# Two layers of cached attention and gated MLP on one core: the first pair's q computed ahead by columns, the softmax scale moved into exp, w_down in 2 KB runs, one more cache unit held, new tables

## The chip, the cores and the metric

The kernel runs on one core of one Trainium2 chip. The metric is the device time of one execution in microseconds; the time before is the median of three runs. A profiled execution of the same program gives the trace. Its engines are called PE (matrix multiply; PEld is its weight load), DVE, ACT, POOL and SP, and SP issues every DMA of this kernel.

## The reference

Four sequences of one token each (B = 4, D = 512) pass twice through the same pair of blocks with the same weights and caches:

```python
x = x + A(layernorm(x)); x = x + B(layernorm(x))     # layer 1
x = x + A(layernorm(x)); x = x + B(layernorm(x))     # layer 2

# A: attention, 32 query heads, 8 cache heads of 4096 x 128
q = (x @ wq).reshape(B, 1, 32, 128).transpose(0, 2, 1, 3)
scores = einsum("bhqd,bhkd->bhqk", q, repeat(k_cache, 4)) * 128 ** -0.5
o = einsum("bhqk,bhkd->bhqd", softmax(scores), repeat(v_cache, 4))
return o.reshape(B, 1, 4096) @ wo
# B: gated MLP, F = 1792
return einsum("bsf,fd->bsd", sigmoid(x @ w_gate) * (x @ w_up), w_down)
```

All inputs are bf16. A cache head of one batch is 1 MB of K and 1 MB of V. The caches are 64 MB in all and do not fit beside the weights, so what layer 2 needs of them is read again unless it was held on the chip.

## The kernel before, in words

**Units and pairs.** A unit is one cache head of one batch in one layer: 2 x 4 x 8 = 64 units. Two neighbouring heads make a pair, so there are 32 pairs. `ORDER` lists the pairs by layer, batch and pair of heads. Pairs of layer 2 of one batch are mixed with pairs of layer 1 of others. Pair g holds units 2g and 2g+1.

**Slots and loads.** Twelve slots of 1 MB hold K or V of a unit. The function `pump` issues the next loads of a fixed list on SP as long as a slot is free (L402), and the parts of the weights wo, w_gate, w_up and w_down in between (L388). `LOADS` sets how K and V alternate in that list. SP takes its list in order, so a load that waits for its slot holds up all behind it. A K slot is given back by the unit's scores, a V slot by its pv. `RET` names, for each batch, heads whose K or V stay in their slots from layer 1 to layer 2 and are not read again: 30 units of 1 MB, so that 98 of 128 cache loads remain.

**A step.** The plan has 33 steps. Step k does the scores and the softmax of pair k and the second product of pair k-1:

- `k_turn` (L848): a unit's K is turned in its slot by a DVE stream transpose, whole (2.3 us) or in halves.
- `q_blocks` (L660, POOL): q of the pair is spread into a block pattern, qz.
- `scores` (L863, PE): 16 matmuls for each unit of the pair. The first unit's are issued in the step before, at the place that `FIRST_AT` names.
- `smax`, `spread_max` (L886, L897), `softmax` (L906 DVE, L914 ACT exp with a bias pointer, L928 POOL), `sums`, `inverse` (L937, L947).
- `ptrans` (L959 PE): the turn of the probabilities, and 16 ACT copies out of PSUM (L982).
- `pv` (L999, PE): 32 matmuls a unit; `normalise` (L1059 DVE); `wo_mm`, `wo_add` (L1077, L1097).

`STEP` holds three small choices for each step: when the first K is turned, whether the first pv goes ahead of the softmax, whether the second K is turned in halves.

**A pass.** When all eight heads of a batch in layer 1 are done, the batch goes through its MLP and on to q of layer 2, while steps of other batches go on. The pass has 18 pieces (`pass_steps`): LayerNorm in three pieces (`ln_a` L507, `ln_b_sum` L573, `ln_b_rs`, the last a Newton iteration for the reciprocal root on DVE), the gate product (`wide_mm`, L676), tanh, the up product, the product of both, `down` (L795), `down_add` (L807), LayerNorm again, then q. q comes as rows: `q_row` (L746), two groups of 16 matmuls with 512 columns; `q_out` brings them out of PSUM with the LayerNorm scale on it (L759 on ACT, L766 on DVE); `q_half` (L776) and `q_turn` (L785) turn them into columns; `q_spread` (L635 PE, L646 ACT) copies them to where POOL reads them. `PLACES` holds one (step, place) for each piece of each batch. A step has nine places, 0 to 8. The last piece also frees the first pair of layer 2: its `q_blocks` is put there, and the first unit's scores at place 8.

**The tail.** After the last pair, all four batches go through the MLP of layer 2 together: `wide_mm` 112 times, `down_rows` (L1299), and one output DMA (L1338).

The weights of `wide_mm` are taken so:

```python
lhsT=wsb[:, k, fc * P:(fc + 1) * P],
```

Of the kernel before, what the change touches and what calls it, by code (L numbers as in the profile page):

```python
# [12 lines left out]


RET = [
    {"k": (0, 5, 6, 7), "v": (4, 5, 6, 7)},
    {"k": (4, 5, 6, 7), "v": (4, 5, 6, 7)},
    {"k": (4, 5, 6, 7), "v": (6, 7)},
    {"k": (0, 1, 2, 6, 7), "v": (0, 1, 6)},
]  # L20

ORDER = [
# [1 line left out]
    (0, 0, (0,)),  # L24
    (0, 0, (2,)),
    (0, 0, (3,)),
    (0, 2, (0,)),
    (0, 1, (1,)),
    (0, 1, (0,)),
    (1, 0, (3,)),  # L30
    (1, 0, (2,)),
    (0, 1, (2,)),
    (0, 1, (3,)),
    (1, 0, (1,)),
    (1, 0, (0,)),
    (0, 2, (1,)),
    (1, 1, (2,)),
    (1, 1, (3,)),
    (0, 2, (3,)),
    (0, 2, (2,)),  # L40
    (1, 1, (1,)),
    (1, 1, (0,)),
    (0, 3, (2,)),
    (1, 2, (3,)),
    (0, 3, (1,)),
    (0, 3, (0,)),
    (0, 3, (3,)),
    (1, 2, (2,)),
    (1, 2, (0,)),
    (1, 2, (1,)),  # L50
    (1, 3, (3,)),
    (1, 3, (0,)),
    (1, 3, (1,)),
    (1, 3, (2,)),
]

PLACES = [
    (
        (1, 8), (2, 0), (2, 0), (2, 0), (2, 0), (2, 0),
        (2, 1), (2, 3), (2, 5), (2, 6), (3, 0), (3, 2),  # L60
        (3, 2), (3, 5), (3, 5), (3, 5), (3, 6), (3, 6),
    ),
    (
        (1, 8), (2, 1), (2, 2), (2, 2), (2, 2), (2, 5),
        (2, 5), (2, 6), (2, 7), (2, 7), (3, 0), (3, 2),
        (3, 2), (3, 2), (3, 5), (3, 5), (3, 6), (3, 6),
    ),
    (
        (1, 8), (2, 0), (2, 1), (2, 2), (2, 2), (2, 2),
        (2, 2), (3, 0), (3, 1), (3, 1), (3, 2), (3, 2),  # L70
        (3, 5), (3, 5), (3, 5), (3, 5), (3, 6), (3, 6),
    ),
    (
        (1, 8), (1, 8), (1, 8), (1, 8), (2, 0), (2, 2),
        (2, 2), (2, 4), (2, 4), (2, 7), (3, 0), (3, 0),
        (3, 0), (3, 0), (3, 0), (3, 2), (3, 5), (3, 5),
    ),
]


FIRST_AT = (
    1, 2, 4, 1, 2, 2, 2, 2,
    2, 2, 2, 2, 2, 8, 7, 2,
    1, 3, 2, 4, 5, 5, 7, 4,
    4, 3, 2, 1, 2, 2, 7,
)

LOADS = (
    "kkvkkk", "", "", "kkvvkkvvvkkv", "kv", "kvk", "vkkvvk", "",
    "kvvvvvkk", "kv", "", "kkkvvkkvv", "k", "kvvkvv", "vk", "",  # L90
    "vkkvkkkkvv", "kkvkvvv", "kvk", "", "kvkvvvvkvvk", "", "kvkv", "",
    "", "kkvkvvkkkkvvkv", "kkvvv", "", "", "vvkkkvkkv", "", "vkvkv",
    "vvv",
)


STEP = (
    9, 3, 4, 9, 3, 9, 7, 0,
    6, 6, 6, 6, 0, 6, 6, 6,
    6, 6, 6, 0, 5, 6, 10, 6,  # L100
    6, 0, 6, 0, 1, 6, 0, 0,
    0,
)


# [101 lines left out]
def bass_interleave_layers__gqa_block_cached__glu_gated_glu__decode_kernel(  # L207
# [17 lines left out]
    P = 128  # L225
# [41 lines left out]
    rm_sb = [[small[:, 6 + 2 * i + t:7 + 2 * i + t] for t in range(2)] for i in range(2)]  # L267
    sm_sb = [[small[:, 10 + 3 * i + t:11 + 3 * i + t] for t in range(3)] for i in range(2)]
    blk_f = small[:, 16:20]
    ones_w = ones_f.broadcast_to([P, P])  # L270
    ident_bf = sbt([P, P], dt.bfloat16, "ident_bf")
    head_b = sbt([P, 2 * REP], dt.bfloat16, "head_b")
# [6 lines left out]
    xc_sb = sbt([P, KD, Bn], dt.float32, "xc")  # L279
    sq_sb = sbt([P, KD + 1, Bn], dt.float32, "sq")  # L280
    newt = sbt([P, 9, Bn], dt.float32, "newt")
    lnsum, _, vpe, nt_a, nt_b, nt_c, nt_y, rs = [newt[:, i, :] for i in range(8)]
    y0i = newt[:, 8, :].bitcast(dt.int32)
    xc_bf = sbt([P, KD, Bn], dt.bfloat16, "xc_bf")
    qT_sb = sbt([P, HQ * Bn], dt.bfloat16, "qT")
    qc_sb = sbt([P, Bn, HKV, NT4, REP], dt.bfloat16, "qc")
# [9 lines left out]
    pidx = qc_f[:, P:P + 32]  # L296
    half_f = qc_f[:, P + 32:P + 64]
    head_s = qc_f[:, P + 64:P + 64 + 2 * REP]
    QC = [f"qc{b}" for b in range(Bn)]
    gs_sb = pe_f[:, 0:KF * Bn]  # L300
    t_sb = pe_f[:, 64:64 + KF * Bn]
    hT_bf = qT_sb[:, 0:KF * Bn].rearrange("p (k b) -> p k b", b=Bn)
# [47 lines left out]
    for k, kinds in enumerate(LOADS):  # L350
        for o in range(2):
# [5 lines left out]
            if 2 * k + o >= 3 and w_small:  # L357
# [9 lines left out]
                         A_wo[n * REP * P:(n + 1) * REP * P, :].rearrange("(h p) n -> p h n", p=P)),  # L367
        "wg": lambda n: (wg_sb[:, n, :], B_w_gate[n * P:(n + 1) * P, :]),
        "wu": lambda n: (wu_sb[:, n, :], B_w_up[n * P:(n + 1) * P, :]),
        "wd": lambda n: (wd_sb[:, n * KH:(n + 1) * KH, :],  # L370
                         B_w_down[n * KH * P:(n + 1) * KH * P, :].rearrange("(k p) n -> p k n", p=P)),
    }
    assert KF == 2 * KH
    wkeys = {"wg": [f"wg{k}" for k in range(KD)], "wu": [f"wu{k}" for k in range(KD)], "wd": ["wd0", "wd1"]}
# [254 lines left out]
    def q_spread(b0, nb):  # L629
        N = HQ * nb  # L630
        fns = []
        for t in range(NT4):
            for a in range(4):
                fns.append(
                    (lambda t, a: lambda e: e.matmul(  # L635
                        M_ps[1][32 * a:32 * a + 32, t * N:(t + 1) * N],
                        lhsT=ident_bf[:, bass.ds(64 * (t // 2) + t % 2, 32, step=2)],
                        rhs=qT_sb[:, 0:N],
                        start=True,
                        stop=True,  # L640
                    ))(t, a)
                )
        S.group("pe", fns, reads=["qT"] + IDENT, writes=["M1"])
        for bi in range(nb):
            act(
                (lambda bi: lambda e: e.activation(  # L646
                    qc_sb[:, b0 + bi, :, :, :],
                    M_ps[1][:, 0:NT4 * N].rearrange("p (t u r b) -> p u t r b", t=NT4, u=HKV, r=REP)[:, :, :, :, bi],
                    ACTF.Copy,
                ))(bi),  # L650
                reads=["M1"],
                writes=[f"qc{b0 + bi}"],
            )

    def q_blocks(g):
        _, b, u = seq[2 * g]
        z = g % 2
        S.inst(
            "pool",
            lambda e: e.tensor_tensor(  # L660
                qz_sb[z][:, :, 0:4 * REP].rearrange("p i (a r) -> p i a r", r=REP),
                qc_sb[:, b, u:u + 2, :, :].rearrange("p u t r -> p (u t) r").unsqueeze(2).broadcast_to([P, 8, 4, REP]),
                blk_f.unsqueeze(1).unsqueeze(3).broadcast_to([P, 8, 4, REP]),
                ALU.mult,
            ),
            reads=[f"qc{b}", "blk"],
            writes=[f"qz{z}"],
        )

    def wide_mm(nb, which, f0, f1, M, mk):  # L670
        wsb, keys = ((wg_sb, wkeys["wg"]), (wu_sb, wkeys["wu"]))[which]
        fns = []
        for fc in range(f0, f1):
            for k in range(KD):
                fns.append(
                    (lambda fc, k: lambda e: e.matmul(  # L676
                        M[:, 64 + fc * nb:64 + (fc + 1) * nb],
                        lhsT=wsb[:, k, fc * P:(fc + 1) * P],
                        rhs=xc_bf[:, k, 0:nb],
                        start=(k == 0),  # L680
                        stop=(k == KD - 1),
                    ))(fc, k)
                )
        S.group("pe", fns, reads=["xcb"] + keys, writes=[mk])
# [71 lines left out]
    def q_out(h):  # L756
        if h == 0:
            act(
                lambda e: e.activation(row_sb[:, :], M_ps[0][:, :], ACTF.Copy, scale=rs[:, 0:1]),  # L759
                reads=["M0", "rs"],  # L760
                writes=["row0"],
            )
        else:
            q_half(0)
            dve(
                lambda e: e.tensor_scalar(row_sb[:, :], M_ps[1][:, :], rs[:, 0:1], None, op0=ALU.mult),  # L766
                reads=["M1", "rs"],
                writes=["row0"],
            )

# [11 lines left out]
    def q_turn():  # L782
        q_half(1)
        dve(
            lambda e: e.tensor_scalar(qT_sb[:, 0:HQ], M_ps[0][:, 0:HQ], RS, None, op0=ALU.mult),  # L785
            reads=["M0"],
            writes=["qT"],
        )
# [26 lines left out]
    def pass_steps(b0):  # L815
# [8 lines left out]
            lambda: down(b0, 1),  # L824
            lambda: down_add(b0),
            lambda: ln_a(b0, 1),
            lambda: ln_b_sum(1),
            lambda: ln_b_rs(1),
            lambda: q_row(0),
            lambda: q_out(0),  # L830
            lambda: q_row(1),
# [70 lines left out]

    def softmax(g):
        p = g % 2
        dve(
            lambda e: e.tensor_tensor_reduce(  # L906
                junk[:, :], MS[:, 0:P], mask_f.rearrange("p s u a h -> p (s u a h)"), rowk_f, BIG,
                ALU.add, ALU.min, nm_sb[p],
            ),
            reads=["MS", "mask0", "mask1", "rowk"],  # L910
            writes=["junk", f"nm{p}"],
        )
        act(
# [2 lines left out]
                S_ps[p][:, 0:2 * P],  # L916
                ACTF.Exp,
                bias=nm_sb[p],
                scale=exp_scale,
                accum_out=sm_sb[p][0],  # L920
            ),
            reads=[f"S{p}", f"nm{p}"],
            writes=["pe0", f"sm{p}"],
        )
        for n in range(2):
# [199 lines left out]
    fresh = {}  # L1125
    for b in range(Bn):
        n = vstep[last[0, b]] - 1
        for (o, w), st in zip(PLACES[b], pass_steps(b)):
            steps.setdefault((n + o, w), []).append(st)
        fresh[1, b] = n + PLACES[b][-1][0]  # L1130
        first = min(pos[1, b, u] for u in range(HKV)) // 2
        assert n + PLACES[b][-1][0] < first, (b, n, first)

    assert all(PLACES[b][0] >= (1, 8) for b in range(Bn))
    spans = sorted((min(kw), max(kw)) for kw in (
# [4 lines left out]
    def do_steps(g, w):  # L1140
        for st in steps.pop((g, w), ()):
            st()
        new = g + 1 < NP and fresh.get(seq[2 * g + 2][:2]) == g
        if new and w == PLACES[seq[2 * g + 2][1]][-1][1]:
            q_blocks(g + 1)
        if g + 1 < NP and w == (8 if new else FIRST_AT[g]):
            scores(g + 1, 0)
            pump()

# [22 lines left out]
    for k, (sg, vg) in enumerate(plan):  # L1172
# [26 lines left out]
            pump()  # L1199
        if vg is not None:  # L1200
            sums(vg)
        if nxt is not None and fresh.get(seq[2 * nxt][:2]) != k:
            q_blocks(nxt)
        do_steps(k, 0)
        turn_at, pv_first, halves = STEP[k] % 3, STEP[k] // 3 % 2, STEP[k] // 6
# [180 lines left out]
```

## Time and profile before

| | |
|---|---|
| median of 3 runs | 314.81 us (314.43 to 315.02) |
| profiled execution | 313.97 us, its span 312.2 us |
| busy, of the span | PE 218.2, PEld 160.2, DVE 174.7, ACT 133.6, POOL 25.8 us |
| DMA | 116.67 MB on the queue that SP feeds, 376 GB/s over the span |
| cache loads | 47 of K and 51 of V, 1024 KB each, median 11.2 and 10.7 us from issue to landing |
| w_down | 2 loads of 896 KB in runs of 1 KB, median 22.2 us from issue to landing |

Busy times count an engine's instructions, not its waits. A matmul's end is modelled, so the spans of matmul groups are better than single durations. GB/s over a stretch shows whether transfers ran without a break; the DMA queue's waits show which engine gave back the slot that a load waited for.

### The profile page before, as it was taken

Reading aid. Unit: us, or ns where it says so; the run is one execution under the profiler, and the core shown is the slowest. Engines: PE = TensorE matmul, PEld = TensorE weight load, DVE = VectorE, ACT = ScalarE, POOL = GpSimd, SP = SyncE. Lnnn points to the kernel's source line nnn. Section 1 sums busy time; section 2 is a strip of 40 time slices with the busy share of each in tenths; the row PEclk is TensorE's granted clock in tenths of the full one; section 3 lists DMA queues with packets and bytes.
Section 4 is the critical chain, followed back from the end, with each engine's and each line's share of the span. In section 5 each row is a group of like instructions: output and inputs, shape, how many; then the busy total and the mean of one; then the engine's idle time right before and its main releaser. Section 6 shows DMA issues by size and latency. Waiting matters only on the chain. (4 is left out here: it accounts for less than half of the span.)

```text
span 312.2 us, 12055 instructions
## 1 busy us (share of the span) xinstructions
PE 218.2 (70%) x5196; PEld 160.2 (51%) x5196; DVE 174.7 (56%) x440; ACT 133.6 (43%) x588; POOL 25.8 (8%) x106
## 2 busy tenths in 40 slices
PE   1326301573349988787998877789777869988886
PEld 0313101352238566466846555665554658466676
DVE  4468220736138457974643995653886548326643
ACT  0022300545041555775156674524555741566730
POOL 0001000000000001100001000000100000020200
PEclk9999999999999999999999999999755555575555
DMA  7999999999998999999999999999999996999900
GB/s 289 427 421 388 384 405 419 422 418 378 390 400 347 415 409 420 420 418 410 352 371 341 421 423 420 418 419 418 419 420 418 417 386 244 389 345 425 401 17 3
DMA packets 21968, 117.43 MB, mean 376 GB/s; under 512 B 1944, under 2 KB 7836, under 8 KB 8860
## 3 DMA queue, kind: packets, MB, share of 16 engines
q1 hardware_dynamic: 21916, 116.67, 93.4%
q8 instruction: 41, 0.67, 0.9%
q14 instruction: 11, 0.09, 0.1%
HBM read 116.66 MB, written 0.00 MB: 374 GB/s over the span
## 5 line engine op out<-in xcount | busy, mean ns | idle before, releaser
L982 ACT ACTIVATE pT<-PT 32x64 bf16<-32x64 f32 x496 | 106.4, 214 | 82.4 <-PE PT L959 71.0
L848 DVE STREAM_TRANSPOSE slot<-slot 128x1024 f32<-128x1024 f32 (+1 forms) x63 | 109.9, 1748 | 24.7 <-DMA slot<-in_A_k_cache_dram 24.5
L999 PE MATMUL O_ps<-pT,slot 128*128 128x4 bf16 x1984 | 63.6, 167 | 43.2 <-DMA slot<-in_A_v_cache_dram 35.1
L999 PEld LDWEIGHTS O_ps<-pT,slot 128*128 128x128 bf16 x1984 | 60.5, 105 | 49.1 <-DMA slot<-in_A_v_cache_dram 35.7
L863 PE MATMUL S_ps<-slot,qz 128*32 128x256 bf16 x1024 | 64.4, 403 | 11.2 <-DVE slot L848 6.5
L863 PEld LDWEIGHTS S_ps<-slot,qz 128*32 128x32 bf16 x1024 | 29.2, 125 | 27.4 <-DVE slot L848 8.3
L914 ACT ACTIVATE pe<-S_ps,small 128x256 bf16<-128x256 f32 x32 | 15.1, 473 | 42.8 <-issue 24.4
L928 POOL TENSOR_TENSOR small<-small 128x1 f32<-128x1 f32 x64 | 12.3, 193 | 238.6 <-ACT pe L914 236.1
L1059 DVE TENSOR_TENSOR oT<-O_ps,rden 128x8 bf16<-128x8 f32 x32 | 5.3, 165 | 37.3 <-PE O_ps L999 36.1
L1077 PE MATMUL O_ps<-oT,wo 128*128 128x2 bf16 (+1 forms) x640 | 20.0, 165 | 6.1 <-DMA wo<-in_A_wo_dram 4.5
L1077 PEld LDWEIGHTS O_ps<-oT,wo 128*128 128x128 bf16 x640 | 18.7, 104 | 7.7 <-issue 6.6
L886 DVE TENSOR_REDUCE small<-S_ps 128x1 f32<-128x256 f32 x32 | 12.9, 404 | 13.2 <-PE S_ps L863 13.2
L906 DVE CUSTOM_DVE_ANT_0 junk<-MS,mask_f,small 128x128 bf16<-128x128 f32 x32 | 10.8, 338 | 11.3 <-PE MS L897 10.3
L897 PE MATMUL MS<-ident_bf,small 128*128 128x128 bf16 x64 | 12.5, 299 | 5.3 <-DVE small L890 5.3
L959 PE MATMUL PT<-ident_bf,pe 128*128 128x128 bf16 x64 | 11.9, 289 | 4.9 <-ACT pe L914 4.9
L660 POOL TENSOR_TENSOR qz<-qc,small 128x128 bf16<-128x128 bf16 x32 | 12.6, 399 | 32.9 <-ACT qc L646 32.9
L746 PE MATMUL M_ps<-wq,xc_bf 128*1 128x512 bf16 x128 | 14.7, 623 | 0.0
L937 PEld LDWEIGHTS MS<-head_b,small 128*128 128x128 bf16 x96 | 5.0, 107 | 12.6 <-issue 12.6
L897 PEld LDWEIGHTS MS<-ident_bf,small 128*128 128x128 bf16 x64 | 4.2, 108 | 14.1 <-DVE small L890 6.6
L1097 DVE TENSOR_TENSOR xT<-xT,O_ps 128x8 f32<-128x8 f32 (+1 forms) x20 | 3.2, 158 | 14.2 <-PE O_ps L1077 14.1
L646 ACT ACT_TABLE_LOAD x1 | 1.3, 1283 | 21.4 <-PE M_ps L635 21.4
L676 PEld LDWEIGHTS M_ps<-xc_bf,wg 128*128 128x128 bf16 x280 | 8.9, 107 | 0.4 <-DVE xc L520 0.4
(83 smaller groups left out, 160.3 us busy)
## 6 DMA issues: line engine op xcount, KB each, us to landing
slot<-in_A_v_cache_dram SPq DMA_DIRECT2D x51, 1024.0 KB, 10.7
slot<-in_A_k_cache_dram SPq DMA_DIRECT2D x47, 1024.0 KB, 11.2
wq<-in_A_wq_dram SPq DMA_DIRECT2D x4, 1024.0 KB, 7.6
wo<-in_A_wo_dram SPq DMA_DIRECT2D x8, 512.0 KB, 14.0
wg<-in_B_w_gate_dram SPq DMA_DIRECT2D x4, 448.0 KB, 10.1
wu<-in_B_w_up_dram SPq DMA_DIRECT2D x4, 448.0 KB, 12.1
wd<-in_B_w_down_dram SPq DMA_DIRECT2D x2, 896.0 KB, 22.2
row<-in_A_x_dram SPq DMA_DIRECT2D x1, 4.0 KB
```

Source lines behind the costliest of these rows:

```text
L660: lambda e: e.tensor_tensor(qz_sb[z][:, :, 0:4 * REP].rearrange("p i (a r) -> p i a r", r=REP), qc_sb[:, b, u:u + 2, :, :].rearrange("p u ...
L746: (lambda k, st: lambda e: e.matmul(M_ps[h][32 * st:32 * st + 1, :], lhsT=xc_bf[:, k, 0:1], rhs=wv[:, k, h, :, st, :], start=(k == 0), sto ...
L848: dve(lambda e: e.transpose(kf, kf), writes=[f"s{st}"])
L863: (lambda t, b2, e_, w0, s: lambda e: e.matmul(S_ps[p][32 * s:32 * s + 8 * REP, 0:2 * P], lhsT=qzf[:, w0:w0 + 8 * REP], rhs=ktv[:, :, s, : ...
L886: lambda e: e.tensor_reduce(m, S_ps[p][:, 0:2 * P], AX.X, ALU.max),
L897: (lambda n, col: lambda e: e.matmul(MS[:, 0:P], lhsT=top(col).broadcast_to([P, P]), rhs=ident_bf[:, :], start=(n == 0), stop=(n == 1)))(n ...
L914: lambda e: e.activation(pe_sb[p].rearrange("p j m -> p (j m)"), S_ps[p][:, 0:2 * P], ACTF.Exp, bias=nm_sb[p], scale=exp_scale, accum_out= ...
L928: (lambda n: lambda e: e.tensor_tensor(sm_sb[p][n + 1], sm_sb[p][n], top(sm_sb[p][n]), ALU.subtract))(n),
L959: (lambda j: lambda e: e.matmul(PT[:, j * P:(j + 1) * P], lhsT=pe_sb[p][:, j, :], rhs=ident_bf[:, :], start=True, stop=True))(j)
L982: (lambda dst, frm: lambda e: e.activation(dst, frm, ACTF.Copy))(dst, frm),
L999: (lambda x, c, j: lambda e: e.matmul(O_ps[p][:, ul * REP:(ul + 1) * REP], lhsT=vv[:, x * JG + c * 2 + j, :], rhs=pT[:, x, j, 2 * c + ul, ...
L1077: (lambda c, r: lambda e: e.matmul(O_ps[p][:, 64 + 2 * c:64 + 2 * c + nb], lhsT=wo_sb[:, u * REP + r, c * P:(c + 1) * P], rhs=oT_sb[n][:, ...
```

## The change

1. **q ahead by columns.** `front[b]` is the pair of heads that comes first in layer 2 of batch b. A new piece `q_first` computes q of its eight heads as columns, 32 matmuls of one column each, from the weights of wq. `q_first_spread` copies them to qc. They are two new pieces, and with them a pass has 20. The other pairs' q comes as before from rows, and `q_spread` leaves out the first pair on its way out of PSUM, so it is one ACT copy or two. The keys of qc are split in two per batch. The first pair's `q_blocks` is placed after `q_first_spread`, the other three pairs' after the last piece at the earliest.
2. **Scale in exp.** In layer 2 q stays without the LayerNorm scale. `exp_scales` makes two columns per batch, and softmax of layer 2 takes them as pointers: one as scale of the exp, one in the reduction that makes its bias.
3. **w_down in runs of 2 KB.** A partition takes two neighbouring rows of w_down instead of one, in parts of 8 and 6 row blocks instead of 7 and 7. To match, `wide_mm` takes every second column of w_gate and w_up as weights.
4. **31 units held** instead of 30: batch 0 nine instead of eight, the other counts are unchanged. 97 cache loads remain.
5. **All tables** (`RET`, `ORDER`, `PLACES`, `FIRST_AT`, `LOADS`, `STEP`) are new. In `LOADS` six K stand ahead of the first V, and the first weight parts come after twelve cache loads instead of six.

```diff
 RET = [
-    {"k": (0, 5, 6, 7), "v": (4, 5, 6, 7)},
+    {"k": (0, 2, 3, 4, 6, 7), "v": (2, 6, 7)},
     {"k": (4, 5, 6, 7), "v": (4, 5, 6, 7)},
     {"k": (4, 5, 6, 7), "v": (6, 7)},
-    {"k": (0, 1, 2, 6, 7), "v": (0, 1, 6)},
+    {"k": (2, 4, 5, 6, 7), "v": (4, 6, 7)},
 ]
...
-        "wd": lambda n: (wd_sb[:, n * KH:(n + 1) * KH, :],
-                         B_w_down[n * KH * P:(n + 1) * KH * P, :].rearrange("(k p) n -> p k n", p=P)),
+        "wd": lambda n: (wd_sb[:, 8 * n:min(KF, 8 * n + 8), :].rearrange("p (j i) n -> p j (i n)", i=2),
+                         B_w_down[8 * n * P:min(KF, 8 * n + 8) * P, :].rearrange("(j p i) n -> p j (i n)", p=P, i=2)),
...
+    def q_first(b):
+        u = front[b]
+        fns = []
+        for r in range(2 * REP):
+            for k in range(KD):
+                fns.append(
+                    (lambda r, k: lambda e: e.matmul(
+                        M_ps[0][:, r:r + 1],
+                        lhsT=wq_sb[:, k, (u * REP + r) * DH:(u * REP + r + 1) * DH],
+                        rhs=xc_bf[:, k, 0:1],
...
+        dve(lambda e: e.tensor_copy(qT_sb[:, 0:2 * REP], M_ps[0][:, 0:2 * REP]), reads=["M0"], writes=["qT"])
...
+    def exp_scales(b):
+        for col, c, key in ((es_sb[b], RS * exp_scale, "es"), (rk_sb[b], -RS * exp_scale, "rk")):
+            dve(
+                (lambda col, c: lambda e: e.tensor_scalar(col, rs[:, 0:1], c, None, op0=ALU.mult))(col, c),
...
-                        lhsT=wsb[:, k, fc * P:(fc + 1) * P],
+                        lhsT=wsb[:, k, bass.ds(2 * P * (fc // 2) + fc % 2, P, step=2)],
...
-                lambda e: e.activation(row_sb[:, :], M_ps[0][:, :], ACTF.Copy, scale=rs[:, 0:1]),
+                lambda e: e.activation(row_sb[:, :], M_ps[0][:, :], ACTF.Copy),
...
-                lambda e: e.tensor_scalar(row_sb[:, :], M_ps[1][:, :], rs[:, 0:1], None, op0=ALU.mult),
+                lambda e: e.tensor_copy(row_sb[:, :], M_ps[1][:, :]),
...
             lambda: ln_a(b0, 1),
+            lambda: q_first(b0),
             lambda: ln_b_sum(1),
-            lambda: ln_b_rs(1),
+            lambda: q_first_spread(b0),
+            lambda: (ln_b_rs(1), exp_scales(b0)),
             lambda: q_row(0),
...
+        es, rk, ek, rkk = (exp_scale, rowk_f, [], "rowk") if l == 0 else (es_sb[b], rk_sb[b], [f"es{b}"], f"rk{b}")
...
-                scale=exp_scale,
+                scale=es,
...
-        if g + 1 < NP and w == (8 if new else FIRST_AT[g]):
+        if g + 1 < NP and w == (max(FIRST_AT[g], new[1]) if new and new[0] == g else FIRST_AT[g]):
             scores(g + 1, 0)
```

The places of batch 3 stand for the others. The 18 pieces before and the 20 after, as (step, place) from the step in which the batch's last pair of layer 1 has its scores; the second LayerNorm begins at the tenth:

```diff
-        (1, 8), (1, 8), (1, 8), (1, 8), (2, 0), (2, 2),
-        (2, 2), (2, 4), (2, 4), (2, 7), (3, 0), (3, 0),
-        (3, 0), (3, 0), (3, 0), (3, 2), (3, 5), (3, 5),
+        (1, 8), (2, 0), (2, 2), (2, 2), (2, 2), (2, 2),
+        (2, 2), (2, 5), (2, 5), (2, 6), (2, 8), (3, 0),
+        (3, 0), (3, 3), (3, 6), (3, 6), (4, 0), (4, 2),
+        (4, 5), (4, 6),
```

## The prediction, made before the changed kernel ran

> **What bounds the kernel now.** I read first the page's busy shares beside its DMA row, then a table by stage, then the DMA queue's own waits, and last the order of one pass between the layers.
>
> ```profile
> PE 218.2 (70%) x5196; PEld 160.2 (51%) x5196; DVE 174.7 (56%) x440; ACT 133.6 (43%) x588; POOL 25.8 (8%) x106
> GB/s 289 427 421 388 384 405 419 422 418 378 390 400 347 415 409 420 420 418 410 352 371 341 421 423 420 418 419 418 419 420 418 417 386 244 389 345 425 401 17 3
> ```
>
> No engine is full, and the loads run at a ceiling of about 420 GB/s with dips. 116.67 MB at 419 GB/s take 278 us of the 312.2; the rest is the start, the dips and some 14 us after the last load. I cut the span where the dips begin and end (columns: stretch, its length, busy time and count of PE, PEld, DVE, ACT, POOL, then granted clock, DMA share, GB/s):
>
> ```profile
> 92.60:103.00 10.40, 9.99 (x280) 8.61 (x283) 7.93 (x25) 1.17 (x6) 0.39 (x2) 1.00 0.93 366
> 103.00:146.00 43.00, 36.12 (x810) 24.75 (x806) 27.91 (x65) 26.56 (x119) 4.82 (x19) 1.00 1.01 417
> 146.00:172.00 26.00, 24.65 (x579) 17.55 (x575) 13.84 (x48) 12.38 (x54) 2.26 (x9) 1.00 0.96 358
> 172.00:253.00 81.00, 64.72 (x1524) 46.25 (x1517) 56.35 (x122) 44.15 (x197) 8.15 (x33) 0.81 1.01 419
> 253.00:259.00 6.00, 4.91 (x130) 4.46 (x134) 2.16 (x14) 3.43 (x16) 0.00 (x0) 0.50 0.88 344
> 259.00:282.00 23.00, 20.69 (x489) 14.84 (x493) 10.76 (x36) 9.84 (x42) 2.22 (x9) 0.57 0.90 334
> 282.00:299.00 17.00, 14.43 (x360) 11.08 (x352) 11.33 (x29) 13.13 (x60) 3.30 (x13) 0.50 0.86 359
> ```
>
> The bound alternates. Where GB/s is 417 to 419 the DMA sets the pace and PE has idle time; where it falls, PE is busy 90 to 96%. The falls are the passes between layer 1 and layer 2 of batches 0, 1 and 3. Against 419 GB/s they cost the DMA 53/419 x 10.4 = 1.3 us, 61/419 x 26 = 3.8 us and 1.1 + 4.7 = 5.8 us. The queue says why:
>
> ```profile
> SPq L199 <- PE O_ps L999: 89.2, 40, 5.9
> SPq L199 <- PE S_ps L863: 62.7, 20, 8.2
> ```
>
> A load is not issued until a slot is given back by the pv (L999) or the scores (L863) that read it last. A pass puts some 10 us of other PE work between two such releases, and the queue runs dry.
>
> The granted clock falls to 0.50 at 222 us without showing in the rows: 196 scores matmuls took 12.31 us in 103 to 146 at 1.00 (63 ns) and 156 took 9.70 in 222 to 253 at 0.50 (62 ns). So I charge added PE work the same everywhere.
>
> The chain that counts goes: loads until 146, PE through batch 1's pass until 172, loads until V of unit 49 lands at 252.9 (issued 244.2, 8.8 us to landing) and its pv starts at once, then PE until 299, and a tail that this change hardly touches.
>
> **The change, term by term** (span 312.2; the profiled execution took 313.97, so 1.8 lies around it; it is 0.8 below the median 314.81).
>
> One unit more held: 97 cache loads, not 98, so 1.049 MB less, 2.5 us at 419 GB/s. Following both programs' orders, from pair 9 on a pair mostly needs one MB less of loads behind it than before, and just as many loads remain behind each release (the last V is issued after the same scores, first half of pair 29, in both). In 172 to 253 the loads set the pace, so it is on the path: **-2.5**. Its price lies early: batch 0 now holds nine units, so the streams have a slot less. K of unit 13 used to be issued after the first half of pair 5's scores (80.4); now it waits for the first half of pair 6's, which stands behind the gate product, about 96. The shortest load in the trace took 4.8 us to land, its turn 2.3, so the second half of pair 6's scores would start near 103.3 instead of 102.8. In SP's order V of units 10 and 11 stand behind it, needed a step later. PE waits some 1.5 us, but has 6.9 us idle in 103 to 146. I count **0** (bounds 0 and +1.5).
>
> w_down in runs of 2 KB: its halves of 0.918 MB land 2.63 and 2.54 us apart behind wo's sixth part (issued at 55.0, 55.5 and 62.8, landing 22.5, 24.6 and 19.8 us later). That is 355 GB/s. At the caches' rate of 419 both take 4.4 instead of 5.2. They stand in the queue ahead of wo's last part, which ends step 4, so they are on the path: between 0 and -0.8, and as w_gate's parts, in 3.5 KB runs, came at about 400 GB/s I take **-0.5**. [...]
>
> q ahead by columns: per batch 32 matmuls like L606's (128 in 3.6 us, 0.9 us) and 16 like L635's (64 in 1.2 us, 0.3 us); no q_row is dropped. So PE gets 1.2 us more per batch, 4.9 in all; DVE gets one 0.19 us copy and two 0.15 us scales, ACT one or two 0.28 us copies. For it, the first layer 2 scores no longer stand behind both q_rows, turns and spread:
>
> ```profile
> 269.02 3.58 PE L746 MATMUL M_ps<-wq,xc_bf 128*1 128x512 bf16 x32
> 274.27 0.28 PE L635 MATMUL M_ps<-qT,ident_bf 128*32 128x32 bf16 x16 [0.28 <-DVE qT L785]
> 275.08 0.76 POOL L660 TENSOR_TENSOR qz<-qc,small 128x128 bf16<-128x128 bf16 x2
> 275.53 0.83 PEld L863 LDWEIGHTS S_ps<-slot,qz 128*32 128x32 bf16 x32
> ```
>
> From LayerNorm's second sum (268.5) to those scores (275.5) went 7.0 us. Now the q_rows lie one or two pairs later. Batch 1: steps 12 and 13 carry about 2 us less each, step 14 3.5 more. Their release times even out, to one every 2 us against 2.5 us of transfer, so the 3.8 us hole should mostly close; but PE does no less there, and its waits for V loads after 92 us sum to only 6.5 us (7 waits of O_ps for in_A_v_cache), with some 4 more for turned K. I take **-2.0** (0 to -3.8). Batch 0's 1.2 us goes into the idle of 103 to 146, batch 2's into that of 172 to 253 (16.3 us): 0 each, +1.2 each if that cover is gone. Batch 3's is in the open: **+1.2**. In its favour, q_row, turns and spread of later pairs can fill waits of PE after 276 (2.6 us idle in 282 to 299, most behind ACT): **-1.0** (0 to -1.5).
>
> Scale in exp: 16 layer 2 exps (L914, 473 ns, its bias already a pointer) get a pointer scale. No row has both. The tanh of 14 columns with a pointer takes 273 ns, the plain copy of 64 columns 214, so 0 to 0.1 us each; nearest is the upper end. ACT lies on the path only in the last four pairs: **+0.4** (0 to +1.6). The first such exp also waits for the Newton steps and two scales on DVE; the tables put these half a step ahead of it, so 0, and if they were late, the 16 copies of the pair's turn (214 ns each) would queue behind it. That q's rows no longer wait for Newton gains nothing: q_row hides that now.
>
> Strided weight loads in wide_mm (every second column): **0**, see the second rival. The rest of the tables moves work without a count that I can price; it widens the range.
>
> Sum: -2.5 - 0.5 - 2.0 + 1.2 - 1.0 + 0.4 = -4.4. Span 307.8, execution 309.6, median **310.4**.
>
> **Rivals.**
>
> 1. *Holes move instead of closing.* Only the MB and w_down count: -2.5 - 0.5 + 1.2 + 0.4 = -1.4, 313.4. For it: that K of unit 13, while SP has nothing it may issue for some 2 us; against it: releases nearer to even in both later passes.
>
> 2. *Strided weights load slower* (the slow side). 560 loads of L676 change from adjacent columns to every second. Now 56 matmuls with loads take 1.6 us, 29 ns each. No row has 128 strided columns; the nearest, L635 with 32 strided columns, shows 106 ns against 104 contiguous, but is short. If the rate halved, 112 each in the tail, batch 3's and batch 1's pass, 336 x 29 ns = 9.7 us, land on the path: 314.8 - 4.4 + 9.7 = 320.1. From 13 ns a load (4.4/336) the gain is gone. [...]
>
> 3. *PE is the bound throughout.* If the earlier data meets no wait of PE, the MB and the holes give nothing, and q ahead costs in batches 0, 1 and 3: -0.5 + 3.6 + 0.4 - 1.0 = +2.5, 317.3. For it: 95% busy in 146 to 172; against: V49's pv starting on its landing, and 16.3 us of idle before it.
>
> 4. *More is gained*: hole closed fully (-3.8), w_down at 419, exp hidden, PE's waits at the end filled (-1.5): -2.5 - 0.8 - 3.8 + 1.2 - 1.5 = -7.4, 307.4.
>
> **How the numbers follow.** Forecast 0.55 (308.5 to 312.5), rival 1 0.17, rival 2 0.08, rival 3 0.12, rival 4 0.08. The range 306 to 316.5 holds the forecast, rivals 1 and 4; it leaves out 2 and most of 3. About 0.2% (0.6 us) is what a measurement tells apart: faster is the forecast, rival 4 and 0.10 of rival 1, together 0.73; same takes 0.05, mostly rival 1; slower 0.22.
>
> **What would show it.** DMA bytes 115.6 MB, 97 cache loads, w_down's two parts nearer 2.3 us per 0.9 MB. V of unit 49 landing near 247 to 249 rather than 252.9. GB/s near 410 in batch 1's pass, and a dip near 95 as before. Scores of pair 28 some 5 us earlier. L676's 56 in 1.6 us. exp near 0.56 us in layer 2. I am wrong if V49 lands no earlier, if PE from there to the end grows by over 3 us, or if L676 exceeds 2 us per 56.

## The result, and the profile after

The changed kernel took 317.63 us (median of 4 runs, 317.12 to 319.38), the kernel before 314.62 beside it. The ratio is 1.0104 with a 95% interval of 1.0061 to 1.0148: slower by 3.0 us, where 4.4 faster was forecast. The profiled execution took 317.12, with a span of 315.3 against 312.2.

From the page of the changed kernel, TensorE's busy time, the DMA rate in 40 slices, and the queues (packets, MB, share of the engines' time):

```profile
PE 220.8 (70%) x5388; PEld 165.0 (52%) x5388; DVE 170.7 (54%) x450; ACT 136.1 (43%) x593; POOL 26.1 (8%) x106
GB/s 293 429 419 422 417 388 390 399 419 339 386 396 278 348 394 356 414 423 421 300 352 384 424 419 419 420 420 415 375 423 418 420 418 223 327 420 420 411 28 3
q1 hardware_dynamic: 20876, 115.62, 92.2%
q8 instruction: 42, 0.69, 0.9%
```

The change does what it says: 192 matmuls more (5388 against 5196), 115.62 MB. Queue 8 was overlooked in the prediction; it becomes the main thing below. The stretches, with the columns of the prediction; the first is the same by the clock, the others are cut at the same events as before:

```profile
92.60:103.00 10.40, 10.15 (x290) 8.97 (x288) 5.20 (x19) 1.67 (x7) 0.39 (x2) 1.00 0.86 305
103.00:149.50 46.50, 39.34 (x910) 27.85 (x911) 26.34 (x69) 26.36 (x117) 4.89 (x19) 0.91 0.98 393
149.50:177.70 28.20, 25.04 (x592) 17.83 (x595) 14.93 (x50) 13.02 (x57) 2.32 (x9) 0.50 0.95 358
177.70:256.70 79.00, 65.60 (x1575) 48.14 (x1567) 54.79 (x126) 44.70 (x197) 7.96 (x33) 0.52 1.01 415
```

The events are: wo's last part landing, batch 1's pass beginning and ending, V of unit 49 landing, the end. TensorE's busy and idle time in each stretch are beside its length (us, before and after):

| stretch | before | after | change | TensorE busy | TensorE idle |
|---|---|---|---|---|---|
| start to wo's last part | 90.7 | 92.2 | +1.5 | 31.1, 30.4 | 59.6, 61.8 |
| to batch 1's pass | 55.2 | 57.3 | +2.1 | 47.6, 49.8 | 7.6, 7.5 |
| batch 1's pass | 25.7 | 28.2 | +2.5 | 24.4, 25.0 | 1.4, 3.2 |
| to V of unit 49 | 81.3 | 79.0 | -2.3 | 65.1, 65.6 | 16.2, 13.4 |
| to the end | 59.3 | 58.6 | -0.7 | 50.1, 50.0 | 9.2, 8.7 |

The MB less shows in the long stretch and the end is a little shorter. What loses is the first 178 us. In batch 1's pass the rate is 358 GB/s as before: the hole did not close. Two early waits of TensorE stand out. One is in its waits (engine, line, waited for: us, times, longest; first the kernel before, then the changed one), the other in its order of time around K of unit 13:

```profile
PE O_ps L999 <- DMA slot<-in_A_v_cache_dram: 35.1, 10, 18.3
PE O_ps L1077 <- DMA wo<-in_A_wo_dram: 4.5, 2, 2.8
```

```profile
PE O_ps L1141 <- DMA wo<-in_A_wo_dram: 25.7, 3, 13.2
PE O_ps L1063 <- DMA slot<-in_A_v_cache_dram: 13.7, 12, 3.7
```

```profile
101.79 1.68 PE L855 MATMUL M_ps<-qT,wd 128*128 128x1 bf16 x56
106.12 1.04 PE L925 MATMUL S_ps<-slot,qz 128*32 128x256 bf16 x16 [2.65 <-DVE oT L1123]
```

```profile
103.75 2.31 DVE L910 STREAM_TRANSPOSE slot<-slot 128x2048 f32<-128x2048 f32 x1 [3.41 <-DMA slot<-in_A_k_cache_dram]
105.99 0.13 DVE L1123 TENSOR_TENSOR oT<-O_ps,rden 128x8 bf16<-128x8 f32 x1
```

wo (25.7 us of waiting, 4.5 before) stands in SP's order behind cache loads. That is not a loss of its size: the waits for V fell by nearly as much, and both together are 39.4 us against 39.6. What is lost there is the 1.5 us by which wo's last part lands later. K of unit 13 was released at the place that the prediction named, landed at 103.73 (98.1 before) and was turned until 106.06; TensorE stood 2.65 us, and DVE's `normalise` (L1123) stood behind the turn.

### The profile page after: what moved, and what is told of

It reads as the page before. It is cut to its first block, busy times and chain, and to the rows that moved or that the text cites. A ratio compares the mean times of both kernels' runs of the same rounds, so it can differ in the third digit from the quotient of the medians.

```text
span 315.3 us, 12445 instructions
## 1 busy us (share of the span) xinstructions
PE 220.8 (70%) x5388; PEld 165.0 (52%) x5388; DVE 170.7 (54%) x450; ACT 136.1 (43%) x593; POOL 26.1 (8%) x106
## 3 DMA queue, kind: packets, MB, share of 16 engines
q1 hardware_dynamic: 20876, 115.62, 92.2%
## 5 line engine op out<-in xcount | busy, mean ns | idle before, releaser
L910 DVE STREAM_TRANSPOSE slot<-slot 128x1024 f32<-128x1024 f32 (+1 forms) x61 | 105.1, 1727 | 8.9 <-DMA slot<-in_A_k_cache_dram 8.9
L1063 PE MATMUL O_ps<-pT,slot 128*128 128x4 bf16 x1984 | 63.5, 166 | 23.3 <-DMA slot<-in_A_v_cache_dram 13.7
L925 PEld LDWEIGHTS S_ps<-slot,qz 128*32 128x32 bf16 x1024 | 30.8, 128 | 32.1 <-DVE slot L910 8.0
L1141 PE MATMUL O_ps<-oT,wo 128*128 128x2 bf16 (+1 forms) x640 | 20.1, 165 | 28.4 <-DMA wo<-in_A_wo_dram 25.7
L978 ACT ACTIVATE pe<-S_ps,small 128x256 bf16<-128x256 f32 x16 | 7.6, 474 | 38.3 <-issue 30.0
L1123 DVE TENSOR_TENSOR oT<-O_ps,rden 128x8 bf16<-128x8 f32 x32 | 5.1, 160 | 28.4 <-PE O_ps L1063 26.7
L978 ACT ACTIVATE pe<-S_ps,small,newt 128x256 bf16<-128x256 f32 x16 | 9.0, 564 | 12.4 <-DVE small L970 5.4
```

Source lines behind the costliest of these rows:

```text
L910: dve(lambda e: e.transpose(kf, kf), writes=[f"s{st}"])
L925: (lambda t, b2, e_, w0, s: lambda e: e.matmul(S_ps[p][32 * s:32 * s + 8 * REP, 0:2 * P], lhsT=qzf[:, w0:w0 + 8 * REP], rhs=ktv[:, :, s, : ...
L978: lambda e: e.activation(pe_sb[p].rearrange("p j m -> p (j m)"), S_ps[p][:, 0:2 * P], ACTF.Exp, bias=nm_sb[p], scale=es, accum_out=sm_sb[p ...
L1063: (lambda x, c, j: lambda e: e.matmul(O_ps[p][:, ul * REP:(ul + 1) * REP], lhsT=vv[:, x * JG + c * 2 + j, :], rhs=pT[:, x, j, 2 * c + ul, ...
L1141: (lambda c, r: lambda e: e.matmul(O_ps[p][:, 64 + 2 * c:64 + 2 * c + nb], lhsT=wo_sb[:, u * REP + r, c * P:(c + 1) * P], rhs=oT_sb[n][:, ...
```

## The experiments

All ratios are to the kernel before, run beside on the same chip. Each version lies at one place in TensorE's stream of instructions; what the place alone is worth comes out under "TensorE's supply of instructions", and differences of one or two per cent between two versions are to be read with that in mind.

### Parts of the change alone

**w_down alone** (`x4_wd`): the kernel before with these two edits.

```diff
-"wd": wd_sb[:, n*KH:(n+1)*KH, :] <- "(k p) n -> p k n"
+"wd": wd_sb[:, 8*n:min(KF,8*n+8), :] <- "(j p i) n -> p j (i n)", i=2
-lhsT=wsb[:, k, fc*P:(fc+1)*P]
+lhsT=wsb[:, k, bass.ds(2*P*(fc//2) + fc%2, P, step=2)]
```

> The kernel before with w_down in 2 KB runs and every second column as weights, nothing else. My term: 0 to -0.8 us, 313.8 to 314.6 us; L676's groups of 56 still 1.6 us. If strided weights were slower: 320 us.

313.80, ratio 0.9989 (0.9967 to 1.0011). In line with the forecast, but not told apart from no change; the 56 gate matmuls with strided weights took 1.63 us as before, so rival 2 is out.

**w_down and the scale in exp** (`x7_scale`): in addition the edits of `q_out`, `q_turn`, `softmax` and `exp_scales`. TensorE's instructions and all tables stay.

> Kernel before with two parts of the change alone: w_down in runs of 2 KB and the scale in exp (two scales on VectorE, a pointer as scale of exp in layer 2, q's rows copied without scale). Tables, units held and TensorE's stream as before. Term by term: 313.8 for w_down alone, plus 0.4 (0 to 1.6) for exp: 314.2, range 313.6 to 315.4. Rival: if the scale in exp carries most of what the code costs under the tables of before, 317 or more; then q ahead is nearly free.

313.48, ratio 0.9967 (0.9942 to 0.9993): a little faster than the kernel before, and 0.1 below the range. The exps do get dearer, here in the costliest groups of this kernel (busy, mean ns | idle before):

```profile
L926 ACT ACTIVATE pe<-S_ps,small,newt 128x256 bf16<-128x256 f32 x16 | 9.0, 565 | 12.6 <-DVE small L918 5.2 <-issue 4.4 <-ACT pT L994 2.8
L926 ACT ACTIVATE pe<-S_ps,small 128x256 bf16<-128x256 f32 x16 | 7.6, 474 | 29.6 <-issue 18.0 <-DVE small L918 9.8 <-ACT pT L994 1.7
```

A pointer as scale costs 91 ns each, and the time does not show it.

**All the code, old tables** (`x1_code`): the changed kernel with `RET`, `ORDER`, `LOADS`, `STEP` and `PLACES` of before, the two new steps put at the place of the second LayerNorm sum, and the first scores of a batch's layer 2 kept behind its pass.

> The new code (q ahead by columns, scale in exp, w_down in 2 KB runs) under the tables of before: 30 units held, same order, q_first and its spread put where the second LayerNorm's sum and Newton steps stood, first scores of layer 2 left at place 8. Theory A (the tables and the ninth unit of batch 0 cost the time, the code is nearly neutral): 313.5 to 316 us, V of unit 49 landing at 252 to 254 us. Theory B (the code costs: 4.9 us more PE work, 16 slower exps): 317 us or more.

321.95, ratio 1.0251 (1.0218 to 1.0285). Theory A falls. The code costs and the new tables win a part back. Between `x7_scale` and this kernel lies only q ahead: +2.8%. A part of it is a wait that the old places make (TensorE's waits in this kernel):

```profile
PE M_ps L813 <- ACT qc L705: 3.6, 3, 1.5
```

q_row writes the bank from which ScalarE still copies the spread.

**The copy on VectorE** (`x6_dve`), to price that wait:

```diff
-act(lambda e: e.activation(qc_sb[:, b, u:u+2], M_ps[0]..., ACTF.Copy))
+dve(lambda e: e.tensor_copy(qc_sb[:, b, u:u+2], M_ps[0]...))
```

> The changed code under the tables of before (321.95), but the spread of q ahead is copied out of its bank by VectorE and not by ScalarE; TensorE's instruction stream stays the same. There three of the four q_rows waited for ScalarE's copy, 3.6 to 4.1 us in all. Theory W (this new wait is most of what the code costs there): 317.5 to 319.5. Rival F (the added instructions move the block ends, and the stalls are most of it): 320.5 to 322.5, since other waits take the place of this one.

319.80, ratio 1.0161 (1.0121 to 1.0200). Between the two theories: the wait is 0.9%, q ahead still costs 1.9% (1.0161 over 0.9967), 6.1 us. Its TensorE time is 4.9 us in four passes, of which I had charged batch 3's 1.2.

**30 units held** (`x2_30`): `RET` of batch 0 without K head 0, so that it is read again.

```diff
-{"k": (0, 2, 3, 4, 6, 7), "v": (2, 6, 7)},
+{"k": (2, 3, 4, 6, 7), "v": (2, 6, 7)},
```

> The changed kernel, but batch 0 holds eight units as before (K of its head 0 is read again): 98 loads. Theory A1 (the missing slot dries the queue between 70 and 136 us): the second half of pair 6's scores no longer waits 2.65 us, the 2.5 us of the extra MB are more than won back, 314.5 to 316.5 us. Rival (the slot is not what costs): 2.5 us slower than the changed kernel, about 320 us.

317.54, ratio 1.0099 (1.0058 to 1.0140). Both theories miss: one MB more costs nothing and wins nothing. With it wo's last part lands at 90.1 and K of unit 13 at 100.0, against 92.2 and 103.7; by V of unit 49 both are level (257.0 and 256.7). So the unit held does cost a slot early, as theory A1 has it. That its net is zero is not shown apart from the stalls treated below: batch 1's pass begins 2.1 us earlier with 30 units (147.3 against 149.5), and then the same pv that stalls 1.07 us in the changed kernel stalls 3.26 us here:

```profile
159.26 0.40 PE L1063 MATMUL O_ps<-pT,slot 128*128 128x4 bf16 x9 [3.26 <-issue]
```

**The head of `LOADS`** (`x5_head`): its first five entries from the kernel before.

```diff
-"kkkkkkvkkvkk", "", "", "vvkvvvkv", "",
+"kkvkkk", "", "", "kkvvkkvvvkkv", "kv",
```

> The changed kernel with the first five entries of LOADS from the kernel before, so the first weight parts come after six cache loads instead of twelve. Theory A1: the 13 us wait of wo_mm in step 2 goes, wo's last part lands near 90.7 instead of 92.2 us, and no more than these 1.5 us are won: 316 to 317.6 us. Theory A2 (the late weights at the start are the main loss, as they hold back the slots of steps 2 and 3): 313 to 315 us.

323.36, ratio 1.0300 (1.0261 to 1.0339). Both theories miss. TensorE's waits for wo do fall, to 5.1 us from 25.7, but those for V rise to 30.3 from 13.7, and wo's last part lands at 96.2, K of unit 13 at 108.0: for the new `ORDER` the new head is the better one, and the wait of 13 us for wo is no loss by itself.

### TensorE's supply of instructions

In `x1_code` one `down` of batch 1's pass took 3.8 us instead of 1.63, with no semaphore behind it; the kernel's order of time there:

```profile
155.58 0.67 PE L862 MATMUL M_ps<-qT,wd 128*128 128x1 bf16 x20
158.29 1.12 PE L862 MATMUL M_ps<-qT,wd 128*128 128x1 bf16 x36 [2.04 <-issue]
```

The trace holds 42 transfers of queue 8 ("instruction"), 16 KB each; in the kernel before 41. 10392 matmuls and weight loads (5196 of each) over 41 are 253 each, 10776 over the changed kernel's 42 are 257. I take each of these transfers for a block of TensorE's stream. A stall here is a time of over 0.45 us from the start of one matmul or weight load to the start of the next that ends on no semaphore; q_row's regular 0.41 of idle time is left out. After 92 us the stalls sum to 7.1 us in the kernel before and to 13.2 in the changed one. Counted in TensorE's stream, neighbouring stalls stand about such a block apart: numbers 7510, 7761, 8013 and 8265 in the changed kernel, 251 or 252 from one to the next. Of the 232 such stalls in all 19 traces here, 229 end 2.2 to 2.7 us after one of these transfers began (median 2.4). After 12 of the changed kernel's 42 transfers a stall ends, and the stalls are 5 to 25 us per execution in the traces here.

**Theory F:** TensorE stands where its stream runs past a block that is not there yet. That it waits for the transfer is my reading of the 2.4 us and of the numbers in the stream; no semaphore shows it. The test moves the work against the block ends, with idle matmuls where TensorE waits for w_q anyway (4.1 us in the kernel before):

```diff
+[matmul(PT[:, 0:4], lhsT=ident_bf, rhs=ident_bf[:, 0:4])] * N     # in q_mm, N = 32, 64, 96, 128
```

> Only 64 small matmuls (128 instructions of TensorE's stream, half of one 16 KB instruction block) are added, in the 4 us of idle time before q of all batches, where TensorE waits for w_q; all later instructions of its stream are moved by half a block against the block ends. Theory F (TensorE stands still where its stream runs into a block that is not there yet, so that the place of the block ends decides which group of matmuls stalls): the stalls that no semaphore explains, 7.1 us after 92 us in the kernel before, fall on other groups and sum to something else, likely more, 9 to 15 us; time 315.5 to 320. Rival N (these stalls belong to the work and not to the place in the stream): 314.0 to 315.2, the same groups stall as before.

> The same 64 matmuls in front of the changed kernel. Theory F: the stalls, 13.2 us after 92 us, fall on other groups; the time moves by more than 0.7 us from 317.6, to either side, 313.5 to 320; by how much it moves against the 64 in the kernel before shows how much of the loss of 3.0 us is luck of the place. Rival N: 317.0 to 318.4, same groups.

> 32 idle matmuls in front of the kernel before, a quarter of a block. If the place of the block ends is luck and the kernel before has a good place among four (0: 314.7, 64: 316.2), this one gives 315 to 318. If the place matters only where many instructions are near the limit of their supply, as in the changed kernel, 314.4 to 315.5.

> 96 idle matmuls in front of the kernel before, three quarters of a block: the same two cases as with 32, 315 to 318 or 314.4 to 315.5. The mean of the four places of the kernel before is what its work takes without the luck of the place: by the first case 315.5 to 316.5, by the second some 315.2.

> 32 idle matmuls, a quarter of a block, in front of the changed kernel. Theory F: another set of groups stalls; the time is anywhere from 315 to 322, and with 0, 64 and 96 it shows the spread that the place alone makes. Rival N: between 317.6 and 322.0 by the number of instructions, about 319.8.

> 96 idle matmuls in front of the changed kernel. With 0, 32 and 64 it gave 317.6, 320.8 and 322.0. If these are luck alone, this one lies anywhere in 314 to 322 and the two means of four places differ by less than 1.5 us. If the change costs by itself, 318 to 322, and the means differ by 3 us or more.

> 128 idle matmuls (256 instructions, one whole block) in front of the changed kernel, where 64 gave 322.0. Theory F: a whole block puts the block ends back on the same work as in the changed kernel: 317 to 318.8, and the stalls stand in the same groups as in its own trace (for instance pv near 126.8 and wo_mm near 245.2). Rival N (more instructions in front cost by themselves): 322 or more.

| idle matmuls | kernel before: us, ratio | stalls | changed: us, ratio | stalls |
|---|---|---|---|---|
| 0 | 314.62, 1 | 7.1 | 317.63, 1.0104 | 13.2 |
| 32 | 317.86, 1.0083 | 9.6 | 320.82, 1.0224 | 18.0 |
| 64 | 316.20, 1.0057 | 10.0 | 322.00, 1.0236 | 25.3 |
| 96 | 313.39, 0.9954 | 5.1 | 316.91, 1.0065 | 22.2 |
| 128 | | | 319.06, 1.0125 | 15.0 |

Three of these times lie outside my ranges: 64 in front of the changed kernel (above 320), 128 there, and 96 in front of the kernel before (below both cases). The place counts: with it the kernel before runs from 0.9954 to 1.0083. In the kernel before and with 64 in front of it, TensorE stalls at the same number in its stream (4219), on other work (first without, then with the 64):

```profile
156.09 0.62 PE L863 MATMUL S_ps<-slot,qz 128*32 128x256 bf16 x8
156.96 0.62 PE L863 MATMUL S_ps<-slot,qz 128*32 128x256 bf16 x8 [0.26 <-issue]
```

```profile
155.74 0.24 PE L802 MATMUL M_ps<-qT,wd 128*128 128x1 bf16 x4
157.35 1.55 PE L802 MATMUL M_ps<-qT,wd 128*128 128x1 bf16 x52 [1.37 <-issue]
```

A whole block more (128) puts 11 of the 12 stalls back into the same groups; its time is the changed kernel's within the intervals, though its median lies 0.3 above the range that I gave. Rival N is out: 96 in front made both kernels faster than 32 or 64.

And yet the place is not why the change lost. At each of the four places the changed kernel is slower, by 1.0, 1.4, 1.8 and 1.1%; the means are 1.0024 and 1.0157, 4.2 us apart. It is the means that differ: at its worst place the kernel before (1.0083) is behind the changed one at its best (1.0065). The sum of stalls does not give the time either: with 96 the changed kernel stalls 22.2 us and is at its fastest. A stall in time that TensorE would have waited for a load anyway need not cost; that was not followed stall by stall.

**Number or time?** Both in `x7_scale`, where q ahead would stand: 48 idle matmuls of 128x4 a pass, or 4 of 128x512.

> The kernel with w_down's runs and the scale in exp alone (313.48), and in each pass, where q ahead would stand, 48 idle matmuls of 128x4 with their weight loads: as many instructions as q ahead (96 a pass, 384 in all, 1.5 blocks of 256), some 1.4 us of TensorE time a pass, and no result that anybody waits for. Theory F (what q ahead costs is instructions, since in dense work a block of TensorE's stream takes 6.1 us to come, however short its matmuls are): 316.5 to 320, and more unexplained stalls than the 5.0 us there. Rival P (it costs its TensorE time): 4 x 1.4 us, in the open in the passes of batches 1 and 3 only: 315 to 316.5, and no more than the next kernel. Rival D (it costs by who waits for its results): 313.5 to 314.5.

> The same place, but 4 idle matmuls of 128x512 a pass: 32 instructions in all where the kernel before this one has 384, and at least as much TensorE time (4 x 0.4 us a pass, 1.6 against 1.4). Theory F: 313.5 to 316, at least 2 us below the 48 small ones. Rival P: as slow as the 48 small ones or slower.

321.17, ratio 1.0208 (1.0173 to 1.0244), and 317.12, ratio 1.0083 (1.0055 to 1.0112). Their groups (matmuls, busy us, mean ns):

```profile
L826 PE MATMUL M_ps<-wq,ident_bf 128*128 128x4 bf16 x192 | 5.7, 166 | 0.0
```

```profile
L826 PE MATMUL M_ps<-wq,ident_bf 128*128 128x512 bf16 x12 | 5.9, 634 | 1.0 <-PE M_ps L509 1.0
```

(Of the 16, 12 records are in the trace.) At no more TensorE time, the kernel with 352 instructions more takes 1.25% longer, 3.9 us; rival P had it no slower. Over `x7_scale` the few cost 1.2% and the many 2.4%, both above theory F's ranges; the many cost no less than q ahead's 1.9%, so nothing that depends on its result is needed to explain it.

This points to the number, but does not prove it. The idle matmuls also move all later work against the block ends, the many by 96 instructions a pass and the few by 8, and the place alone moved the kernel before by 1.3%. In the profiled executions the q rows of batches 0 to 3 begin 1.2, 5.3, 6.6 and 6.7 us later with the many than in `x7_scale`, and 1.7, 2.9, 3.3 and 3.6 us later with the few. Most of the difference arises on the way to batch 1's q rows, where one stall stands. In the kernel with many, `down` of batch 1's pass stalls behind the same 20 matmuls as in `x1_code`, where as many instructions stand in front:

```profile
155.53 0.67 PE L805 MATMUL M_ps<-qT,wd 128*128 128x1 bf16 x20
158.86 1.10 PE L805 MATMUL M_ps<-qT,wd 128*128 128x1 bf16 x36 [2.65 <-issue]
```

**Fewer under the new tables** (`x8_thin`):

```diff
 def q_first(b):
-            for k in range(KD):
+            for k in range(1):
```

> The changed kernel with q ahead's matmuls cut from 32 to 8 a pass: it sums only the first of four parts of x, so that its q is wrong. 192 instructions less in all (0.75 block) and some 0.7 us of TensorE time less a pass; all waits, copies and loads as in the changed kernel. If q ahead's instructions cost under the new tables as they do under the old ones (6 us for 384): 313.5 to 316. If by TensorE time in the open alone (batch 3's pass, half of batch 1's): 316 to 317. If it is hidden now: 317.3 to 318; the place of the block ends behind each pass moves as well and may add 2 to either side.

319.18, ratio 1.0143 (1.0105 to 1.0182). A miss: 192 instructions less, and if anything slower, with 24.7 us of stalls. Each pass moves all behind it by 48 instructions, so other groups stall. What q ahead's instructions alone cost under the new tables stays open.

**The best of both** (`s96_scale`): `x7_scale` with 96 idle matmuls in front.

> The two versions below the kernel before put together: w_down in runs of 2 KB with the scale in exp (0.9967 of the kernel before) and 96 idle matmuls in front (0.9954). If the two add: 0.992, about 312.2. If the better place is luck of one set of times and does not carry over: 313 to 315.5.

313.25, ratio 0.9964 (0.9938 to 0.9991). They do not add, but this version, `x7_scale` and the kernel before with 96 in front (0.9928 to 0.9979) all beat both kernels.

## Why the prediction was wrong

By stretches the sum said -0.5 to wo's last part (w_down), 0 to batch 1's pass, -2.0 in it, -2.5 to V of unit 49 and +0.6 from there to the end. Measured were +1.5, +2.1, +2.5, -2.3 and -0.7. So the long stretch came as forecast, and nearly all of the miss lies ahead of it. The sign that was named for being wrong came too: V of unit 49 landed at 256.7, not before 252.9.

1. **The hole of batch 1's pass**, -2.0 forecast, was +2.5; this step failed worst. The releases are more even, but the pass still holds both q_rows, and q ahead on top, for which the sum has no term of its own in this pass. TensorE is busy 0.7 us longer and idle 1.8 us longer. In the idle time, one pv stalls 1.07 us in its middle with no semaphore behind it (before, the one such stall took 0.26), and two waits are new: 0.45 us for a V load, and 0.60 for ScalarE's copies of the probabilities, which were turned right behind the stalled pv (the changed kernel's order of time, with q ahead and the two q_rows):

```profile
156.74 0.78 PE L1063 MATMUL O_ps<-pT,slot 128*128 128x4 bf16 x23 [0.45 <-DMA slot<-in_A_v_cache_dram]
158.58 0.40 PE L1063 MATMUL O_ps<-pT,slot 128*128 128x4 bf16 x9 [1.07 <-issue]
163.18 0.38 PE L1063 MATMUL O_ps<-pT,slot 128*128 128x4 bf16 x8 [0.60 <-ACT pT L1046]
164.45 1.01 PE L671 MATMUL M_ps<-xc_bf,wq 128*128 128x1 bf16 x32 [0.23 <-DVE xc_bf L526]
169.21 1.88 PE L806 MATMUL M_ps<-wq,xc_bf 128*1 128x512 bf16 x16
172.20 1.88 PE L806 MATMUL M_ps<-wq,xc_bf 128*1 128x512 bf16 x16
```

2. **The cover for q ahead** failed in one of the two places that the prediction named: "Batch 0's 1.2 us goes into the idle of 103 to 146, batch 2's into that of 172 to 253 (16.3 us): 0 each". Batch 2's did: the long stretch has 0.5 us more of busy TensorE, and its idle time shrank by 2.8. Batch 0's did not. On the way to batch 1's pass TensorE is busy 2.2 us longer, 1.3 of it q ahead and 1.0 a wo_mm that the new order puts there, and its idle time stays at 7.5 us. Some waits of the kernel before went, but the 2.65 us for K of unit 13 and 2.3 us of stalls (1.7 before) keep it full.

   What such idle time is worth may depend on the supply. Between two transfers of queue 8, in stretches where the loads ran at 415 GB/s or more, lay never under 5.8 us (246 intervals of all traces after 92 us, a tenth under 6.0); under 350 GB/s it went down to 3.3. By my estimate from this 5.8 us and the 253 matmuls and weight loads for each transfer, TensorE got at full load one matmul with its weights every 46 ns at most. The kernel before used one every 53 ns in 172 to 253 (81 us for 1524), so by that estimate 13% was left there on the mean, less in the dense groups; the changed one uses one every 50. I had priced a small matmul at its 29 ns (56 in 1.63 us).

3. **The unit held**, -2.5: right in its stretch (-2.3), wrong in its price, counted 0 (to 1.5). The second half of pair 6's scores began at 106.1, where I had worked out 103.3, and TensorE waited 2.65 us for it, not 1.5. `x2_30` has K of unit 13 3.7 us earlier and wo's last part 2.1, which I had not followed at all. The two kernels end level, with the stalls said above between them.

4. **Right:** the strided weights (56 matmuls in 1.63 us, as before), the pointer's price (91 ns, and hidden) and 97 loads. w_down alone is in line, though no run tells it from 0; the end (+0.6 forecast, -0.7 measured) is near.

Under the old tables the parts come, by ratios, to -0.33% for w_down and scale, +1.94 for q ahead and +0.90 for its bank's wait; the new tables with the unit held then take 1.47 back, to the +1.04 of the change. Each of these is measured at one place, and by up to 1.7% they may be luck of the place. What stands at all four places is that the change as a whole costs, 1.3% on the mean. How that divides between q ahead, the tables and the unit held is open.

Rival 3, "PE is the bound throughout", gave 317.3 and had 0.12. That its number fits is in part luck: it put the MB at nothing, which showed (-2.3), and it has no loss ahead of wo's last part (+1.5). Its view of batch 1's pass is the nearer one, but it lacks the stalls: TensorE is busy there for 25.0 of 28.2 us, and one pv stalls 1.07 us besides. A sign was in the trace of before: 41 transfers of queue 8 at 6 us (the median from one to the next after 92 us is 6.1) are 246 of 312 us.

## What to carry to other kernels

Count TensorE's instructions as well as its time. Beside loads at 415 GB/s or more, small matmuls came here, by the estimate above, no faster than one in some 46 ns with the weights over a whole block; the 29 ns are those of one group of 56, less than half a block. Idle time of a stretch is cover only if no new wait moves into it: one stretch here took q ahead for nothing, another did not. Before a change is judged by one time, move its work by half a block with idle matmuls: an unrelated shift moved these kernels by 1.3 to 1.7%, as much as most edits.

## What was unexpected in the hardware

- TensorE stalls of 0.5 to 3.4 us without a semaphore, 229 of 232 ending 2.2 to 2.7 us after a 16 KB transfer of queue 8 began. The number in the stream went with the place of a stall (4219 in the kernel before, with 64 idle matmuls in front and without), not with its length: the pv of batch 1's pass stalls 1.07 us in the changed kernel and 3.26 in `x2_30`.
- These transfers came no closer than 5.8 us apart where the loads ran at 415 GB/s or more, and down to 3.3 us apart where they ran under 350. That the loads themselves hold them up is argued from this, not tried.
- The granted clock was 0.50 from 149.5 to 177.7 and 0.52 from there to 256.7 in the changed kernel, 1.00 from 145.9 to 171.6 and 0.81 from there to 252.9 in the kernel before; rows of the same kind agree, such as 16 scores in 1.04 us at 153.44 in the changed one and at 148.92 in the one before.
